# Attention, a gated feed-forward and a Fourier mix in one kernel: other PSUM slots in attention, another order of its first loads and copies, and a second pass without one-column matmuls

## The chip, the cores and the metric

The kernel runs on one core of a Trainium2 chip. The metric is the time of one execution on the device in microseconds (us), smaller being better. The engines are named as in the profile: PE is the matrix engine (TensorE), PEld its weight loads, DVE is VectorE, ACT is ScalarE, POOL is GpSimd, SP is the engine that issues most transfers. PSUM, into which PE writes, has eight banks here, and the kernel's PSUM tiles take one bank each.

## The reference

Three layers follow each other, with B, H, S, DH = 4, 12, 448, 64 and D = 768.

```python
scores = np.matmul(q, k.transpose(0, 1, 3, 2)) / np.sqrt(64) - np.log(S)
x = np.matmul(1.0 / (1.0 + np.exp(-scores)), v)         # then (B, S, D)
xk = mu_k * x + (1 - mu_k) * x_prev                     # x_prev: one token earlier
xr = mu_r * x + (1 - mu_r) * x_prev
kk = np.maximum(xk @ w_k, 0.0)                          # D -> 1024
x = sigmoid(xr @ w_r) * (kk * kk @ w_v)
u = x + np.real(np.fft.fft(np.fft.fft(x, axis=1), axis=2))
un = (u - mean(u)) / np.sqrt(var(u) + 1e-6)
out = u + np.maximum(un @ w_ch1, 0.0) @ w_ch2           # D -> 3072 -> D
```

## The kernel before, in words

The kernel writes one instruction order for every engine by hand. A planner (class `Order`) runs Python generators against a modelled clock `o.now`: a matmul adds its modelled cost to the clock, other engines have a modelled time at which they are free, and a generator that yields a time is resumed when the clock has come there. What a generator issues while it runs is the next instruction of its engine, and at run time each engine works through its list in that order, waiting where data or a buffer is missing. `o.others()` makes all generators that are due run before the calling one goes on, and lets no queued matmul in. Matmuls of the large products are put into `o.feed`, from which the planner takes one whenever no generator is due.

Attention works on 24 pairs of heads (`pairs`, six for each batch; `WHOLE` is 6). Per pair, `scores` makes seven PSUM tiles of 128 keys by 448 queries: six half blocks (numbers 0 to 5, contraction over 64 rows, so that two can share the array) and one full block (`FULL`, number 6). Each gets a sigmoid on ACT (`weigh`). One period later `attnv` adds up the values of the pair into one PSUM tile `av` (14 instructions of fp32 matmul), and `join` copies it to `x` on ACT, stores it, and makes from it the inputs of the key product (`mix`: an ACT scaling, a DVE step, an ACT cast `xkh`, a DVE subtraction `xkl`). Pairs 0 to 5 use fp32 matmuls for the scores; from pair 6 on q and k are split into two parts (`qh`, `ql`, `kh`, `kl`) and three fp32r matmuls make a block. Between the pairs, from pair 8 on, the key product of finished batches is fed in (`keys`, tiles of 18 matmuls, read by ACT's Relu, a square and a cast in `key_done`); a pace of 10.8 modelled us per pair leaves room for it. The planner issues `join` 0.2 modelled us after the last value matmul at the earliest; a score pair of fp32r matmuls is planned at 0.107 each.

PSUM slots turn in order of allocation: a tile waits until the last reader of the tile that had its slot is done. Before the change `ps1` has three slots, shared by key tiles, value sums and full blocks (`bank`), and `ps2` has five, for the half blocks (`room`). After attention `ps2` is given up and five slots (`ps1b`, `bank2`) take its place; `bank` goes on with its three slots.

The first transfers all go out on SP: `mu_k`, then k, q and v of pair 0, then the first weight and pair 1 (`load_mu`, `prepare`, `weights`).

The last layer's network runs over batches 0 and 1 first and then, in a second pass, over batches 2 and 3 together (`pair1`): for each of 12 groups of hidden units seven products of nine matmuls each, X, Y, Z, W, X, Z, W, in four PSUM tiles, and then the second matrix for both batches. In even groups the first product is preceded by an fp32 matmul over one column (`one` in `step`), into a column that nothing reads.

Of the kernel before, what the change touches and what calls it, by code (L numbers as in the profile page):

```python
# [12 lines left out]
F32 = mybir.dt.float32  # L13
# [4 lines left out]
PSUM = bass.MemoryType.PSUM  # L18
# [227 lines left out]
def build(tc, ap):  # L246
    nc = tc.nc
# [4 lines left out]
    def pool(stack, name, bufs=1, side="left", space=None):  # L252
        if space is not None:
            return stack.enter_context(tc.tile_pool(name=name, bufs=bufs, space=space))
        return stack.enter_context(tc.tile_pool(name=name, bufs=bufs, side=side, reuse_waits="tile"))
# [73 lines left out]
    t_d = {(nm, d): dram.tile([128, 2, S], F32, name=f"t_d{nm}{d}") for nm in LATE for d in range(3)}  # L329
    rs_d = [dram.tile([1, S], F32, name=f"rs_d{b}") for b in range(B)]  # L330

    ps1 = pool(est, "ps1", 3, space=PSUM)

    def bank(name):
        return ps1.tile([128, 512], F32, tag="bank", name=name)


# [3 lines left out]
    mop = pool(s_l, "mop", 2, "left")  # L341
    shift(mop, "mop")
    att = pool(s_r, "att", 2, "right")
    ps2 = pool(s_ps, "ps2", 5, space=PSUM)

    bias_s = wkp.tile([128, 1], F32, name="bias_s")
    V.memset(bias_s, -math.log(S))
# [8 lines left out]
    def prepare(what):  # L356

        for i, (b, p) in enumerate(pairs):
            if i > 1:
                yield from o.issued(("av", i - 2) if what == "v" else (what, i - 2) if i - 2 >= WHOLE else ("pair", i - 2))  # L360
            shape = {"k": [128, 4, 128], "q": [128, S], "v": [128, 4, 2, DH]}[what]
            raw = att.tile(shape, F32, tag=what, name=f"{what}_{i}", bufs=2)
            t = o.dma(raw, ap[what][b, p])
            if what == "v" or i < WHOLE:
                pair_t[what, i] = raw
                o.at[what, i] = t
                yield t
            else:
                yield t
                if i > WHOLE + 1:  # L370
                    yield from o.issued(("pair", i - 2))
                if what == "q" and i == WHOLE:
                    shift(att, "att")
                hi, lo = (att.tile(shape, F32R, tag=what + x, name=f"{what}{x}_{i}", bufs=2) for x in "hl")
                pair_t[what, i] = hi, lo
                yield o.act(hi, raw)
                o.at[what, i] = t = o.sub(V, lo, raw, hi)
                yield t
# [6 lines left out]
    def weigh(i, n, ps):  # L385
        sg = att.tile([128, S], F32, tag="sg", name=f"sg_{i}_{n}", bufs=len(places) + 1)
        o.at["sg", i, n] = o.act(sg, ps[:, 0:S], AF.Sigmoid, bias=bias_s, scale=1.0 / math.sqrt(DH))
        sg_t[i, n] = sg

    def scores(i):  # L390
        k, q = pair_t["k", i], pair_t["q", i]

        def rows(j):
            return slice(0, 128) if j is None else slice(64 * j, 64 * j + 64)

        def room(n):
            name = f"sc_{i}_{n}"
            return bank(name) if n == FULL else ps2.tile([128, 512], F32, tag="sc", name=name)

        if i < WHOLE:  # L400
            for n in [FULL, *range(FULL)]:
                c, j = places[n]
                ps = room(n)
                o.mm(ps[:, 0:S], k[rows(j), c], q[rows(j)], True, True, 0.760 if j is None else 0.447)
                weigh(i, n, ps)
                yield from o.others()
        else:
            halves = [(2 * c, 2 * c + 1) for c in range(3)]
            for ns in [(FULL,), *halves] if i < WHOLE + 2 else [*halves, (FULL,)]:
                ps = {n: room(n) for n in ns}  # L410
                for t, (a, b) in enumerate(((0, 0), (0, 1), (1, 0))):
                    for n in ns:
                        c, j = places[n]
                        cost = None if j is None else 0.107
                        o.mm(ps[n][:, 0:S], k[a][rows(j), c], q[b][rows(j)], t == 0, t == 2, cost)
                for n in ns:
                    weigh(i, n, ps[n])
                yield from o.others()
        o.at["pair", i] = o.now

    def attnv(i, ps):
        v = pair_t["v", i]
        for n in [FULL, *range(FULL)]:
            yield from o.need(("sg", i, n))
            c, j = places[n]
            sg = sg_t.pop((i, n))
            if j is None:
                o.mm(ps[:, 0:S], v[:, c].rearrange("p j d -> p (j d)"), sg, True, False, 0.760, skip=True)
            else:
                me = slice(64 * j, 64 * j + 64)  # L430
                o.mm(ps[me, 0:S], v[:, c, j], sg, False, c == 2, 0.432, skip=True)
            yield from o.others()
        o.at["av", i] = o.now
        o.spawn(join(i, ps), o.now + 0.2)
# [23 lines left out]
    def load_mu(mu, src):  # L458

        o.dma(mu[:, 0], src)  # L460
        o.ts(mu[:, 1], mu[:, 0], -1.0, 1.0, ALU.mult, ALU.add)

    def attention():
        for i in range(len(pairs) + 1):
            t0 = o.now
            if i > 0:
                yield from o.need(("v", i - 1), ("sg", i - 1, FULL))
                if i > 2:
                    yield from o.issued(("mixed", i - 3))
                yield from attnv(i - 1, bank(f"av_{i - 1}"))  # L470
            if i < len(pairs):
                yield from o.need(("k", i), ("q", i))
                yield from scores(i)
            yield t0 + pace()
        yield from o.need(("xk", B - 1, NP - 1))
        o.at["attention"] = o.now
# [55 lines left out]
        for part, every in zip((w_parts[:NF], w_parts[NF:]), EVERY):  # L532
            yield from load_split(att, part, raws=2, vector=True, every=every)

    load_mu(mu_k, ap["mu_k"])
    for what in "kqv":
        o.spawn(prepare(what))
    o.spawn(attention())
# [6 lines left out]


    ps1b = pool(est, "ps1b", 5, space=PSUM)

    def bank2(name):
        return ps1b.tile([128, 512], F32, tag="bank2", name=name)  # L550
# [599 lines left out]
    def network():  # L1150
# [31 lines left out]
        def pair1(g, _):  # L1182

            ps, t = {}, {}

            def tmp(nm):
                t[nm] = ws2.tile([128, S], F32, tag=nm, name=f"{nm}_{g}", bufs=1)
                return t[nm]

            def after(n):  # L1190
                x, y, z, w = (ps[k][:, 0:S] if k in ps else None for k in "XYZW")
                if n == 0:
                    o.at["c1", g] = o.act(tmp("u2"), x)
                elif n == 1:
                    yield from o.need(("c1", g))
                    o.at["u2", g] = o.tt(V, t["u2"], t["u2"], y, ALU.add)
                elif n == 2:
                    yield from o.need(("u2", g))
                    o.at["u3", g] = o.tt(V, tmp("u3"), t["u2"], z, ALU.add)
                elif n == 3:  # L1200
                    yield from o.need(("u3", g))
                    o.at["c22", g] = o.tt(V, t["u3"], t["u3"], w, ALU.add)
                    yield o.at["c22", g]
                    yield from hidden(g, 3, 1, t["u3"])
                elif n == 4:
                    yield from hidden(g, 2, 0, x)
                elif n == 5:
                    o.at["c21", g] = o.tt(V, tmp("c21"), t["u2"], z, ALU.add)
                    yield o.at["c21", g]
                    yield from hidden(g, 2, 1, t["c21"])  # L1210
                else:
                    yield o.tt(V, t["u2"], t["u2"], w, ALU.add)
                    yield from hidden(g, 3, 0, t["u2"])
                yield o.now

            def step(n, i, lhs, rhs, k):
                if i == 0 and n < 4:
                    ps[k] = (bank2 if k == "Y" else bank)(f"f1_{g}_{k}")
                if n == 0 and i == 0 and g % 2 == 0:
                    one = (ps[k][:, 511:512], lhs.bitcast(F32), rhs[:, 0:1].bitcast(F32))  # L1220
                    o.mm(*one, True, True, cost=0.2, skip=True)
                o.mm(ps[k][:, 0:S], lhs, rhs, i == 0 and n < 4, i == 8, skip=True)
                if i == 8:
                    o.at["prod", 7 * g + n] = o.now
                    o.spawn(after(n), o.now + 0.1)

            for n, (_, rows, k) in enumerate(PRODUCTS):
                blk = blk_t.get(7 * g + n)
                yield from o.need(("blk", 7 * g + n))
                yield from o.need(*((key, g) for key in {4: ["c1"], 5: ["u3"], 6: ["c22"]}.get(n, [])))  # L1230
                blk = blk_t[7 * g + n]
                for d in range(3):
                    yield from o.need(("t", rows, d))
                    ws = [blk[:, c : c + 128] for c in (128 * d, D // 2 + 128 * d)]
                    rs = [t_t[rows, d][:, c] for c in range(2)]
                    for i, (a, c) in enumerate(((0, 0), (0, 1), (1, 0))):
                        o.feed.append(partial(step, n, 3 * d + i, ws[a], rs[c], k))
                while len(o.feed) > 6:
                    yield o.now + 0.1
# [124 lines left out]
```

## Time and profile before

| | |
|---|---|
| runs before | 1208.70, 1209.18, 1209.23 us; median 1209.18 |
| the profiled execution | 1210.05 us, of which the span of the trace is 1208.3 |
| PE busy | 1198.8 us, 99% of the span, 6142 matmul records |
| DVE, ACT, POOL busy | 894.3, 483.0 and 53.8 us |
| DMA queue of SP | 214.37 MB, busy for 51.5% of 16 engines' span |
| attention and the keys behind it | PE's first matmul at 4.9 us to 282.4 us |
| receptance, values, spectrum, first pass | 282.4 to about 879 us |
| second pass | about 879 us to the end |

A row of the timeline gives the start and the time of an instruction (or of several alike, x n), its engine, its line, the operation, what it writes and reads with shapes, and in square brackets the idle time of its engine ahead of it and what ended that. Line numbers such as L181 are those of the planner's helpers, so groups are told apart by the names of tiles: `sc` scores, `sg` their sigmoids, `av` value sums, `x` their copies, `k` key tiles, `kt` what Relu and square make of them, `f_X` to `f_W` the products of the second pass. Matmuls are pipelined and their ends are modelled, so starts are more telling than ends: in a steady stream one starts every 0.20 us.

### The profile page before, as it was taken

The numbers are of one execution on the slowest core, as the hardware profiler recorded it, in microseconds if no ns is written. First come the engines' busy times: TensorE is split into PE (matmuls) and PEld (weight loads), VectorE is DVE, ScalarE is ACT, GpSimd is POOL, SyncE is SP. The second block draws the span as 40 slices with busy tenths as digits, with TensorE's granted clock in tenths as the row PEclk, the third lists the DMA queues.
The fourth block names the chain that finished last, engine by engine and source line by source line (L and its number), as shares of the span: only waits on it lengthen the run. The fifth ranks groups of instructions, "written<-read, shape, count | busy, mean of one in ns | idle before, by whom it ended". The sixth has DMA issues, their size and how long they took to land.

```text
span 1208.3 us, 16376 instructions
## 1 busy us (share of the span) xinstructions
PE 1198.8 (99%) x6142; PEld 1048.8 (87%) x6142; DVE 894.3 (74%) x1465; ACT 483.0 (40%) x864; POOL 53.8 (4%) x57
## 2 busy tenths in 40 slices
PE   8999999999999999999999999999999999999998
PEld 3467677689999999999999999999999999999998
DVE  5676887656862668797999989899567776777654
ACT  5877677657640121242333333333133332222320
POOL 0000000000000000000000000000021111211110
PEclk9999999999999999999999999999999999999999
DMA  6657569766957555386556555744942112121102
GB/s 213 215 181 233 199 234 349 258 228 237 302 204 246 199 168 199 120 292 239 188 198 212 199 206 196 244 172 177 366 144 79 53 53 79 53 69 63 53 1 92
DMA packets 77295, 217.81 MB, mean 180 GB/s; under 512 B 9312, under 2 KB 31776, under 8 KB 76576
## 3 DMA queue, kind: packets, MB, share of 16 engines
q1 hardware_dynamic: 76544, 214.37, 51.5%
q0 software_dynamic: 672, 2.40, 0.6%
q8 instruction: 48, 0.79, 0.3%
q14 instruction: 31, 0.25, 0.1%
HBM read 143.84 MB, written 72.90 MB: 179 GB/s over the span
## 4 chain that ended last, share of the span: by engine, by line
PE 98%; DMA 1%; ACT 0%; issue 0%; SPq 0%; DVE 0%
PE f L181 43%; PE k L181 10%; PE v L181 9%; PE r L181 7%; PE sc L181 7%; PE av L181 6%; PE f_X L181 4%; PE f_W L181 4%; PE f_Z L181 4%; PE f_Y L181 2%; PE pq L181 1%; DMA k<-k_d 1%; PE pa L181 1%; PE qa L181 1%; PE var L181 0%; DMA q<-in_q 0%
## 5 line engine op out<-in xcount | busy, mean ns | idle before, releaser
L216 DVE TENSOR_TENSOR acc<-acc,f 128x448 f32<-128x448 f32 x258 | 157.3, 617 | 60.3 <-PE f L181 57.6
L181 PE MATMUL f<-un,w1h 128*128 128x448 f32 x576 | 163.7, 364 | 0.0
L181 PE MATMUL f<-h,w2h 128*128 128x448 f32 x576 | 162.8, 363 | 0.0
L181 PE MATMUL f<-h,v2h 128*128 128x448 f32 x576 | 162.2, 362 | 0.0
L235 ACT ACTIVATE sg<-sc,bias_s 128x448 f32<-128x448 f32 x168 | 95.2, 651 | 61.0 <-PE sc L181 61.0
L224 DVE SCALAR_TENSOR_TENSOR w_bits<-w_raw,w_bits 128x768 uint32<-128x768 uint32 (+1 forms) x120 | 114.5, 954 | 1.7
L181 PEld LDWEIGHTS f<-un,w1h 128*128 128x128 f32 x576 | 108.1, 188 | 7.3 <-issue 0.4
L181 PEld LDWEIGHTS f<-h,w2h 128*128 128x128 f32 x576 | 108.0, 188 | 7.3 <-DVE acc L216 0.3
L181 PEld LDWEIGHTS f<-h,v2h 128*128 128x128 f32 x576 | 108.0, 188 | 6.9
L181 PE MATMUL v<-k,wvh 128*128 128x448 f32 x384 | 112.3, 366 | 0.6 <-DMA k<-k_d 0.6
L181 PE MATMUL f<-h,v2l 128*128 128x448 f32 x288 | 104.1, 361 | 0.0
L181 PE MATMUL f<-un,w1l 128*128 128x448 f32 x288 | 103.9, 361 | 0.0
L181 PE MATMUL f<-h,w2l 128*128 128x448 f32 x288 | 103.8, 360 | 0.0
L181 PE MATMUL av<-sg,v 128*64 128x448 f32 (+1 forms) x336 | 81.0, 549 | 0.0
L216 POOL TENSOR_TENSOR v2l<-v,v2h 128x768 fp32r<-128x768 f32 x24 | 46.4, 1950 | 748.5 <-ACT v2h L233 748.5
L181 PEld LDWEIGHTS v<-k,wvh 128*128 128x128 f32 x384 | 71.6, 188 | 6.6 <-DMA k<-k_d 1.3
L181 PE MATMUL v<-k,wvl 128*128 128x448 f32 x192 | 70.1, 365 | 0.0
L181 PE MATMUL k<-xkh,wkh 128*128 128x448 f32 x192 | 69.9, 364 | 0.0
L181 PE MATMUL k<-xkl,wkh 128*128 128x448 f32 x192 | 69.7, 363 | 0.0
L181 PE MATMUL k<-xkh,wkl 128*128 128x448 f32 x192 | 69.5, 362 | 0.0
L181 PEld LDWEIGHTS av<-sg,v 128*64 128x64 f32 (+1 forms) x336 | 27.8, 143 | 43.0 <-issue 36.5
L235 ACT ACTIVATE w_raw<-w_raw 128x768 f32<-128x768 f32 x40 | 36.8, 920 | 58.4 <-DVE w_bits L224 45.8
(174 smaller groups left out, 2254.2 us busy)
## 6 DMA issues: line engine op xcount, KB each, us to landing
w_raw<-in_w SPq DMA_DIRECT2D x40, 768.0 KB, 4.6
w_d<-w_bits SPq DMA_DIRECT2D x40, 384.0 KB, 2.6
k_d<-kp SPq DMA_DIRECT2D x32, 448.0 KB, 2.8
k<-k_d SPq DMA_DIRECT2D x32, 448.0 KB, 6.0
a<-w_d SPq DMA_DIRECT2D x24, 384.0 KB, 3.6
v<-w_d SPq DMA_DIRECT2D x24, 384.0 KB, 3.1
k<-in_k SPq DMA_DIRECT2D x24, 256.0 KB, 5.3
v<-in_v SPq DMA_DIRECT2D x24, 256.0 KB, 3.0
```

What stands on the lines that cost most here:

```text
L181: self.nc.tensor.matmul(out, lhs, rhs, start=start, stop=stop, skip_group_check=skip)
L216: eng.tensor_tensor(out, a, c, op=op)
L224: self.nc.vector.scalar_tensor_tensor(out, a, scalar, c, op0=op0, op1=op1)
L235: self.nc.scalar.activation(out, a, fn, **kw)
```

## The change

Three parts. In attention, PSUM is split as two slots (`ps1`) and six (`ps2`) and not three and five. The full blocks of pairs 6 to 23 and the value sums of pairs 6 to 23 go to the six; those of pairs 0 to 5 stay in the two, with the key tiles. After attention a one-slot pool `ps1c` gives `bank` its third slot back, and every third call of `bank` uses it. In pairs 6 to 23, `scores` calls `o.others()` once more, between the matmuls of blocks 0 and 1 and their sigmoids. At the start, q of pair 0 is issued on ACT's queue, and `mu_k` is loaded by a generator that is due at 2.5 modelled us, not before everything else. In the second pass the one-column matmuls are left out.

```diff
-    ps1 = pool(est, "ps1", 3, space=PSUM)
+    ps1 = pool(est, "ps1", 2, space=PSUM)
+    ps1c = []
+    banked = [0]
     def bank(name):
+        banked[0] += 1
+        if ps1c and banked[0] % 3 == 0:
+            return ps1c[0].tile([128, 512], F32, tag="bankc", name=name)
         return ps1.tile([128, 512], F32, tag="bank", name=name)
...
-    ps2 = pool(s_ps, "ps2", 5, space=PSUM)
+    ps2 = pool(s_ps, "ps2", 6, space=PSUM)
...
-            t = o.dma(raw, ap[what][b, p])
+            t = o.dma(raw, ap[what][b, p], nc.scalar if what == "q" and i == 0 else None)
...
+    def slot(name):
+        return ps2.tile([128, 512], F32, tag="sc", name=name)
...
-            return bank(name) if n == FULL else ps2.tile([128, 512], F32, tag="sc", name=name)
+            return bank(name) if n == FULL and i < WHOLE else slot(name)
...
                         o.mm(ps[n][:, 0:S], k[a][rows(j), c], q[b][rows(j)], t == 0, t == 2, cost)
+                if ns[0] == 0:
+                    yield from o.others()
                 for n in ns:
                     weigh(i, n, ps[n])
...
-                yield from attnv(i - 1, bank(f"av_{i - 1}"))
+                yield from attnv(i - 1, (bank if i <= WHOLE else slot)(f"av_{i - 1}"))
...
-    load_mu(mu_k, ap["mu_k"])
+    def first_mu():
+        load_mu(mu_k, ap["mu_k"])
+        yield o.now
+
+    o.spawn(first_mu(), 2.5)
...
     ps1b = pool(est, "ps1b", 5, space=PSUM)
+    ps1c.append(pool(est, "ps1c", 1, space=PSUM))
...
-                if n == 0 and i == 0 and g % 2 == 0:
-                    one = (ps[k][:, 511:512], lhs.bitcast(F32), rhs[:, 0:1].bitcast(F32))
-                    o.mm(*one, True, True, cost=0.2, skip=True)
```

## Rows read from the trace of the kernel before

**Rows 1.** The page: busy time of an engine, share of the span, instructions.

```profile
PE 1198.8 (99%) x6142; PEld 1048.8 (87%) x6142; DVE 894.3 (74%) x1465; ACT 483.0 (40%) x864; POOL 53.8 (4%) x57
```

**Rows 2.** Table by stage: stretch, its us, busy us per engine, PEclk, DMA share, GB/s.

```profile
0.00:10.00 10.00, 5.11 (x12) 2.35 (x14) 0.32 (x3) 3.07 (x4) 0.34 (x6) 1.00 0.75 238
120.00:160.00 40.00, 40.00 (x213) 27.53 (x213) 34.37 (x50) 28.26 (x57) 0.67 (x4) 1.00 0.58 196
160.00:200.00 40.00, 40.00 (x213) 29.04 (x212) 32.33 (x45) 30.04 (x59) 0.74 (x4) 1.00 0.88 307
251.60:282.40 30.80, 30.80 (x155) 28.88 (x155) 18.05 (x31) 20.61 (x39) 0.00 (x0) 1.00 0.65 241
581.00:879.00 298.00, 298.00 (x1492) 279.03 (x1491) 262.79 (x391) 100.97 (x147) 1.07 (x1) 1.00 0.62 218
```

**Rows 3.** Chain that ended last, pair 12: start, us, what.

```profile
113.46 3.22 PE sc L181 x21
116.67 5.01 PE k L181 x25
```

**Rows 4.** Timeline of PE's matmuls, scores of pair 12.

```profile
114.11 0.36 PE L181 MATMUL sc<-qh,kh 64*128 64x448 f32 x2
...
114.71 0.75 PE L181 MATMUL sc<-qh,kh 64*128 64x448 f32 x2
...
115.79 0.47 PE L181 MATMUL sc<-qh,kh 128*128 128x448 f32 x1
```

**Rows 5.** Timeline of weight loads: values of pair 6, scores of pairs 7 and 12.

```profile
56.20 0.28 PEld L181 LDWEIGHTS av<-sg,v 128*64 128x64 f32 x2 [0.47 <-ACT sg L235]
...
60.32 0.18 PEld L181 LDWEIGHTS sc<-qh,kh 64*128 64x128 f32 x1 [0.57 <-ACT sg L235]
...
114.99 0.18 PEld L181 LDWEIGHTS sc<-qh,kh 64*128 64x128 f32 x1 [0.30 <-ACT sg L235]
```

**Rows 6.** Who waited for whom, 60 to 251 us: total, times, longest.

```profile
PEld sc L181 <- ACT sg L235: 5.3, 17, 0.6
```

**Rows 7.** Timeline of ACT, first sigmoids of pair 12.

```profile
114.30 1.16 ACT L235 ACTIVATE sg<-sc,bias_s 128x448 f32<-128x448 f32 x2 [3.66 <-PE sc L181]
...
115.35 0.53 ACT L233 COPY x<-av 128x448 f32<-128x448 f32 x1
```

**Rows 8.** Timeline of all engines, a boundary between key tiles.

```profile
131.29 0.58 ACT L235 ACTIVATE kt<-k 128x448 f32<-128x448 f32 x1
...
131.89 0.36 PE L181 MATMUL k<-xkh,wkh 128*128 128x448 f32 x1
```

**Rows 9.** Timeline of all engines, the start and pair 2.

```profile
0.74 0.38 SPq L239 DMA_DIRECT2D mu_k<-in_mu_k  x1
...
0.95 1.28 ACT L235 ACT_TABLE_LOAD   x1 [0.95 <-DVE bias_s L347]
1.18 0.42 SPq L239 DMA_DIRECT2D k<-in_k  x1
1.65 0.42 SPq L239 DMA_DIRECT2D q<-in_q  x1
...
4.89 6.48 PE L181 MATMUL sc<-q,k 128*128 128x448 f32 x14 [4.89 <-DMA q<-in_q]
...
8.31 0.34 PEld L181 LDWEIGHTS sc<-q,k 64*128 64x128 f32 x2 [0.41 <-issue]
...
9.05 0.46 PEld L181 LDWEIGHTS sc<-q,k 64*128 64x128 f32 x2 [0.41 <-issue]
...
23.14 0.19 PEld L181 LDWEIGHTS sc<-q,k 64*128 64x128 f32 x2 [0.18 <-issue]
...
23.51 0.19 PEld L181 LDWEIGHTS sc<-q,k 64*128 64x128 f32 x2 [0.18 <-issue]
```

**Rows 10.** Chain that ended last, first products of groups 2 and 3.

```profile
926.03 2.03 PE f_X L181 x11
...
953.28 1.80 PE f_X L181 x9
```

## The prediction

> **What bounds the kernel now.** I read the busy table first: TensorE (PE) is busy for 1198.8 of 1208.3 us [rows 1]. So time comes back only if PE gets fewer instructions, starts earlier, or stands still less between instructions; the reader should see that the last kind can hide in "busy", because a matmul that is held up is drawn long. The table by stage says where to look [rows 2]: in the attention stage PE counts as fully busy, with VectorE (DVE) at 34.37 of 40 us and the DMA engines at 0.88 at their worst, so neither is full. The chain of waits then gives the score step of one pair as 3.22 us and the key feed between pairs as 25 matmuls in 5.01 us, so 0.20 each [rows 3].
>
> The score step is 18 half-height matmuls, which run two at a time, and 3 full ones. At 0.20 a step that is 12 steps, 2.4 us, plus what the changes of array shape cost. PE's timeline [rows 4] shows where the rest goes. Blocks 2 and 3 take 0.60 (114.11 to 114.71). Blocks 4 and 5 start at 114.71, but the next shape begins only at 115.79, 1.08 later. The weight loads tell why: the load for block 5 stood 0.30 us and was released by a sigmoid [rows 5]. Six half blocks turn through five slots, so block 5 takes the slot of block 0 of the same pair, and ScalarE (ACT) began block 0's sigmoid only at 114.30 [rows 7]. The list of waits has this wait 17 times from 60 to 251 us, 5.3 us in all [rows 6]: 16 pairs at 0.30 and pair 7 at 0.57 [rows 5].
>
> **The score slots, part by part.** In pairs 8 to 23 a pair now puts eight tiles through six slots: value sum, blocks 0 to 5, full block. Block 5 reuses the value sum's slot and the full block reuses block 0's. Block 5 is due at about 114.71. The copy of the value sum, which stood behind two sigmoids at 115.35 and took 0.53 [rows 7], is now put ahead of them: the planner resumes whatever is due at the new `others()`, and the copy's generator is due 0.2 after the last value matmul, while the first score pair is planned at 0.64. The value matmuls end about 113.46 [rows 3] and ACT then sat idle until 114.30 [rows 7], so the copy fits before the first sigmoid (113.46 + 0.53 = 114.0) and delays nothing; without that idle time it would push block 0's sigmoid by up to 0.53. The full block is due about 115.4 and block 0's sigmoid ends near 114.9, some 0.5 to spare. So the stall goes and no other takes its place in this step.
>
> What a stall is worth: at least the 0.30 that the load stood, at most 1.08 - 0.60 = 0.48, of which part is the change of shape that stays. I take 0.40, about the middle. Sixteen pairs: 6.4, between 4.8 and 7.7. Pair 7 stood 0.57 and is followed by keys, so PE can use the time: with the same 0.10 on top, 0.67. In pair 6 the value matmuls behind the scores wait for their sigmoids (0.47 in one load [rows 5]); ACT sets the pace there, and I give nothing. Pairs 0 to 5 keep full block and value sum in the two other slots: each pair's two tiles find the slots of the pair before, whose readers are done, so nothing. Attention together: 7.07.
>
> **Two slots for keys.** Keys had three slots together with value sums and full blocks, and now have two alone. Tile t+2 waits for the first ACT pass (Relu) over tile t. A tile is 18 matmuls (3.6 us) and a feed is 25, so only if a boundary falls in the first 7 matmuls of a feed does a third tile begin in the same feed: 7 of 18, some 6 feeds; elsewhere value sums and scores lie between. Behind the last pair the keys run on without a break, but there ACT is busy 20.61 of 30.80 us with no sigmoids ahead of Relu [rows 2], so nothing. The tightest one I found: Relu at 131.29 for 0.58, so done at 131.87, and the tile two later began at 131.89 [rows 8]. It is late because it queues behind the seven sigmoids and the casts. Taking the 0.53 copy out of that queue while PE gains 0.40 leaves it 0.13 better off; but an earlier copy also lets one more cast of the key inputs, about as long as that Relu, get ahead of it. Cost: nothing at best, 6 x 0.58 = 3.5 at worst. I take 0.4, one such wait, since only the tightest has no slack.
>
> **The start.** SP issues `mu_k` at 0.74, k at 1.18 and q at 1.65; PE's first matmul waited for q until 4.89, 3.24 after its issue [rows 9]. With `mu_k` behind v and q on ACT's own queue, k and q both go out near 0.74. With the same 3.24, PE starts at 3.98, 0.91 earlier. ACT's table load stood at 0.95 with nothing before it; q's issue is ahead of it in program order, and the first sigmoid is far off, so the load moves under cover. If the table load went first, q would leave at 0.95 + 1.28 = 2.23, 0.58 later than now: that is the bound below nothing. The SP loads behind q move up by one or two issues of about 0.45; no PE wait hangs on them. PE does not use the whole gain. Over 0 to 10 us the granted clock is listed as 1.00 [rows 2], yet weight loads step 0.74 there (8.31 to 9.05) against 0.37 later (23.14 to 23.51) [rows 9], the rate of the 1.2 GHz level against the 2.4 GHz one. If the end of the slow steps stays where it is, 0.91 is spent at half rate and is worth 0.45; if it moves with the start, 0.91. I take 0.6. The Trainium skill (TensorE: Matmul & The Clock Gate, Part 1, "What's actually happening") says that the cold stretch is a matter of time and not of a number of matmuls, and varies from run to run; by it I would take nearer 0.91 and the sum would be 0.3 larger. One trace cannot show it.
>
> **One-column matmuls.** In the second pass the first product of an even group is 11 instructions in 2.03 us where that of an odd group is 9 in 1.80 [rows 10]. The fp32 matmul over one column is the two more: 0.23 each, six groups, 1.38 us, on PE's path with no waits around it. Bounds: 0 if a wait takes their place, 1.38 if none does; I take 1.38, as the odd groups run without. The Trainium skill (TensorEngine Tiling (Array Packing), "Instruction Overhead") gives a one-column matmul the latency of a 60-column one, some 60 cycles; two of them at 2.4 GHz would be an estimated 0.05 us, six pairs 0.3, and the sum would be 1.1 smaller. The row includes their weight loads and decides.
>
> **Third slot of the later stages.** Every third call goes to the one-slot pool, two of three to the other: the same turn of three slots, so nothing, in either direction. The order of the later work follows PE's, so a shift of its start carries to the end.
>
> **Sum.** 7.07 + 0.6 + 1.38 - 0.4 = 8.65. The profiled execution took 1210.05 (span 1208.3 and 1.75 around it) and comes to 1201.4; the runs' median, 0.87 lower, comes to 1200.5.
>
> **Rivals.**
> - *The wait moves to ACT's queue.* Block 5 and the full block now hang on the copy and on sigmoid 0, keys on Relu. For: attention has only some idle ACT time, and a cast that waits for a load would, if pulled ahead of sigmoid 0, hold everything behind it. Against: 3.66 us of idle ACT ahead of the sigmoids in the pair read [rows 7]. If half the stalls come back and keys cost 1.3: 3.5 + 0.6 + 1.38 - 1.3 = 4.2, 1205.0.
> - *The score gain is not kept:* DVE or the loads set the attention stage and the stalls only covered for them. Against: DVE 34.37 of 40, which a 0.40 shorter 11.4 us pair makes 35.6. Then 0.6 + 1.38 = 2.0 is left: 1207.2.
> - *Slower: two key slots.* If Relu came late in all 6 feeds, the gain of 9.05 is eaten at 1.5 us a feed. Four ACT passes (two casts of the scores' inputs, scaling, cast of the key inputs) of about 0.6 could get ahead of Relu, 2.4 in all: 6 x 2.4 = 14.4 lost, 1209.18 - 9.05 + 14.4 = 1214.5. It needs all four ahead where most already are.
> - *The one-column matmuls keep the clock up.* Against: 298 us of the first pass without any, at 1.00 [rows 2]. Each us at the lower level costs 0.5; eating 8.65 needs 17 us of it.
> - *More than forecast:* all bounds at their best, 7.7 + 0.67 + 0.91 + 1.38 = 10.7: 1198.5.
>
> **How the numbers follow.** Forecast (1198.5 to 1203): 0.67. Wait moved (1203 to 1206.7): 0.18. Gain not kept (about 1207, within 0.2%): 0.05. Slower by keys or clock: 0.06. Still faster than 1198.5: 0.04. A measurement of this kernel tells 0.2%, 2.4 us, from no change. So faster 0.89, same 0.05, slower 0.06. The forecast's own bounds: 10.7 at best, and 4.8 + 0.57 - 0.58 + 1.38 = 6.2 at worst, 1203.0. To hold 8 in 10 it reaches into the first rival: 1198.0 to 1205.0.
>
> **What would show it.** Right: the score step of pairs 8 to 23 in 2.8 us, no load of scores released by a sigmoid, the copy ahead of the first sigmoid, key matmuls 0.20 apart across tile boundaries, PE's first matmul near 4.0, every first product 1.80. Wrong: a weight load of block 5 or the full block waiting for the copy or a sigmoid, a key load waiting for Relu, first matmul at 5 or later, slow steps in the second pass, or DVE full through attention.

## The result, and the profile after

Six runs of the changed kernel gave a median of 1199.85 us (1199.50 to 1200.44), six of the kernel before on the same chip 1209.51 (1208.70 to 1210.97): a ratio of 0.9919, with a 95% interval of 0.9907 to 0.9932. The forecast was 1200.5. The profiled execution took 1199.81 (span 1198.0) where that of before took 1210.05 (1208.3), so the two spans differ by 10.3 and the medians by 9.7. What may have made the 0.6 between them is told with the start of the kernel, below.

The busy table of the page after answers to [rows 1]: PE is still 99% of the span, and the 10 us are missing from its own busy time, not from its idle time.

```profile
PE 1188.8 (99%) x6130; PEld 1043.9 (87%) x6130; DVE 894.2 (75%) x1465; ACT 484.8 (40%) x864; POOL 54.0 (5%) x57
```

The table by stage, for stretches that answer to [rows 2]. DVE and the DMA engines carry the same work in less time; in the 40 us from 120 they rise to 35.86 us and to 0.67 and are still not full. The last row is the second pass: without its one-column matmuls it keeps a granted clock of 1.00.

```profile
0.00:10.00 10.00, 5.49 (x15) 2.15 (x15) 1.79 (x5) 3.72 (x6) 0.34 (x6) 1.00 0.79 273
120.00:160.00 40.00, 40.00 (x223) 29.97 (x224) 35.86 (x51) 33.00 (x64) 0.29 (x3) 1.00 0.67 223
...
870.20:1197.00 326.80, 324.05 (x1620) 303.33 (x1618) 222.94 (x374) 87.02 (x160) 45.51 (x24) 1.00 0.20 65
```

The chain that ended last, after (start, us, what). It answers to [rows 3, 9, 10]: the score step of pair 12 is 2.82 where it was 3.22, the key feed behind it is unchanged, the score step of pair 2 is 3.41, and the first product of the first even group of the second pass is 9 instructions in 1.80.

```profile
0.74 3.73 DMA q<-in_q
4.51 5.47 PE sc L181 x14
9.99 3.35 PE av L181 x14
...
20.17 3.41 PE sc L181 x14
...
43.92 4.36 PE av L181 x14
48.27 2.82 PE sc L181 x21
...
55.43 2.82 PE sc L181 x21
...
108.96 2.82 PE sc L181 x21
111.78 5.01 PE k L181 x25
...
122.77 5.12 PE k L181 x25
...
870.17 1.80 PE f_X L181 x9
```

The same chain before, where it is read below: the scores of pairs 2 and 5, the values of pair 5, the scores of pair 7 from 57.69 to 61.19.

```profile
21.78 3.65 PE sc L181 x14
...
42.78 4.17 PE sc L181 x14
46.95 3.59 PE av L181 x14
...
57.69 0.84 PE sc L181 x3
...
61.19 3.61 PE k L181 x17
```

And from its weight loads the one in pair 5 that stood 0.47 for a sigmoid:

```profile
45.93 0.29 PEld L181 LDWEIGHTS sc<-q,k 64*128 64x128 f32 x2 [0.47 <-ACT sg L235]
```

The timeline of pair 12 after, beside [rows 4, 5, 7]. The copy of the value sum now runs at 109.33, ahead of the first sigmoid at 109.80. Blocks 4 and 5 load both their weights at 110.01 without a wait, run two at a time from 110.20, and the full block begins at 110.91: 0.71 behind them, where it was 1.08. The 0.30 that is left ahead of the full block's load has no releaser; it is the change of array shape. The copy began 0.37 us behind the scores, not at once, and ended as the first sigmoid began; that one came 0.84 behind the start of the scores, as before. So the copy fitted, with less to spare than the prediction says.

```profile
109.33 0.54 ACT L233 COPY x<-av 128x448 f32<-128x448 f32 x1 [3.08 <-PE av L181]
109.80 2.74 ACT L235 ACTIVATE sg<-sc,bias_s 128x448 f32<-128x448 f32 x5
110.01 0.19 PEld L181 LDWEIGHTS sc<-qh,kh 64*128 64x128 f32 x2
110.20 0.37 PE L181 MATMUL sc<-qh,kh 64*128 64x448 f32 x2
110.90 0.19 PEld L181 LDWEIGHTS sc<-qh,kh 128*128 128x128 f32 x1 [0.30 <-issue]
110.91 0.47 PE L181 MATMUL sc<-qh,kh 128*128 128x448 f32 x1
```

The list of waits from 60 to 251 us, after (who, for whom: total, times, longest). The row of [rows 6], loads of scores waiting for a sigmoid, is gone. One load of scores waited for a copy and one load of keys for Relu (`kt`), each once. The load is the first one of pair 22, behind keys; 0.30 is what the full block's load above stands too, with no releaser, and the score step of that pair is 2.83, so nothing was lost by it.

```profile
PEld sc L181 <- ACT x L233: 0.3, 1, 0.3
...
PEld k L181 <- ACT kt L235: 0.2, 1, 0.2
```

**The account.** Cutting both chains at the same pieces of work gives where the 10.3 us of span came from:

| stretch (before, after) | before | after | gain |
|---|---|---|---|
| start to the value sums of pair 0 | 11.37 | 9.99 | 1.38 |
| to the scores of pair 6 (50.54, 48.27) | 39.17 | 38.28 | 0.89 |
| scores and values of pair 6, scores of pair 7 (61.19, 58.25) | 10.65 | 9.98 | 0.67 |
| to the keys behind the last pair (251.60, 242.63) | 190.41 | 184.38 | 6.03 |
| those keys (282.41, 273.44) | 30.81 | 30.81 | 0.00 |
| receptance to the first pass (878.97, 870.17) | 596.56 | 596.73 | -0.17 |
| second pass, to the end of the span | 329.33 | 327.83 | 1.50 |

One pair of traces holds some scatter; the twelve traces of this document tell more. From the value sums of pair 0 to the end of the keys, the three kernels with the old slots and the old copy take 270.99 to 271.04 us, and the four with the new slots, the copy ahead and the casts as they were 263.40 to 263.45: 7.6 for the slots and the call together, where the forecast had 7.07 less 0.4. The new slots without the copy ahead take 268.92, the copy ahead with the old slots 271.51. The second pass takes 329.29 to 329.33 in three traces with one-column matmuls and 327.83 to 327.92 in nine without. The stretch between the two, where the kernels differ only in the pools of their three `bank` slots, takes 596.39 to 597.82 (596.49 to 597.01 with the old slots), so -0.17 is scatter, and part of the scatter of the medians comes from there.

### The profile page after: what moved, and what is told of

Its sections match the earlier page's. It is cut to its first block, busy times and chain, and to the rows that moved or that the text cites. A ratio compares the mean times of both kernels' runs of the same rounds, so it can differ in the third digit from the quotient of the medians.

```text
span 1198.0 us, 16329 instructions
## 1 busy us (share of the span) xinstructions
PE 1188.8 (99%) x6130; PEld 1043.9 (87%) x6130; DVE 894.2 (75%) x1465; ACT 484.8 (40%) x864; POOL 54.0 (5%) x57
## 4 chain that ended last, share of the span: by engine, by line
PE 98%; DMA 1%; ACT 0%; DVE 0%; issue 0%; SPq 0%
PE f L181 43%; PE k L181 10%; PE v L181 9%; PE r L181 7%; PE av L181 6%; PE sc L181 6%; PE f_X L181 4%; PE f_Z L181 4%; PE f_W L181 4%; PE f_Y L181 2%; PE pq L181 1%; DMA k<-k_d 1%; PE pa L181 1%; PE qa L181 1%; PE var L181 0%; DMA q<-in_q 0%
```

## The experiments

| kernel | median, us | before beside it | ratio, 95% interval |
|---|---|---|---|
| slots without the copy moved ahead | 1205.73 | 1209.76 | 0.9969 (0.9959 to 0.9980) |
| copy ahead, old slots | 1210.43 | 1209.76 | 1.0007 (0.9997 to 1.0017) |
| one-column matmuls out, nothing else | 1208.55 | 1209.76 | 0.9990 (0.9980 to 0.9999) |
| new start, nothing else | 1209.40 | 1209.76 | 1.0000 (0.9991 to 1.0010) |
| changed kernel, q on SP | 1200.41 | 1209.34 | 0.9924 (0.9909 to 0.9939) |
| changed kernel, `mu_k` first | 1200.47 | 1209.34 | 0.9926 (0.9911 to 0.9941) |
| changed kernel, casts on DVE | 1198.65 | 1209.34 | 0.9914 (0.9899 to 0.9928) |
| changed kernel, matmuls of zeros first | 1198.46 | 1209.34 | 0.9908 (0.9892 to 0.9925) |
| casts on DVE and matmuls of zeros | 1196.85 | 1210.26 | 0.9893 (0.9878 to 0.9908) |
| the same, q on SP | 1197.61 | 1210.26 | 0.9893 (0.9877 to 0.9910) |

**The slots without the copy ahead.** The changed kernel without its new `o.others()`.

```diff
-                if ns[0] == 0:
-                    yield from o.others()
                 for n in ns:
```

> The changed kernel without the new others() call, so the value sums share the six score slots but are copied behind the first two sigmoids as before. Theory (a slot's last reader decides): from pair 8 on block 5 waits for the copy, which stands behind two sigmoids and ends about 2.5 us after the scores begin; the score step grows from 2.82 to about 4.1 us, 16 pairs lose some 1.3 us each, about 1220 us, slower than before. Rival (the sixth slot alone pays, the order of the copy is a detail): score step 2.82, about 1200 us. In pairs 1 to 5, whose scores use six slots as well, both expect the score step of the changed kernel, 3.41 us and not 3.65.

The score steps of pairs 8 to 21 took 3.20 to 3.21, those of pairs 22 and 23 took 2.82 and 2.81; so neither 4.1 nor 2.82 for all. Those of pairs 1 to 5 took 3.40 to 3.41, as expected. In the timeline of pair 12 of this kernel, block 5's load at 112.53 is still released by a sigmoid, and the copy begins only at 112.90 and ends at 113.44:

```profile
111.85 1.16 ACT L235 ACTIVATE sg<-sc,bias_s 128x448 f32<-128x448 f32 x2 [3.65 <-PE sc L181]
...
112.53 0.18 PEld L181 LDWEIGHTS sc<-qh,kh 64*128 64x128 f32 x1 [0.29 <-ACT sg L235]
...
112.90 0.54 ACT L233 COPY x<-av 128x448 f32<-128x448 f32 x1
...
113.34 0.19 PEld L181 LDWEIGHTS sc<-qh,kh 128*128 128x128 f32 x1 [0.31 <-ACT sg L235]
```

Block 5 at 112.53 and the full block at 113.34 both began before the copy had ended, so neither took the value sum's slot; block 5 still hung on sigmoid 0. That contradicts what the text ahead of the prediction says, that slots turn in order of allocation, and neither expectation came true. What fits is that a slot is handed on in the order in which the last readers are issued: without the new call the first two sigmoids are issued ahead of the copy, and blocks 0 and 1 are first in line. The banks in the programs built from the kernels bear it out: in pairs 8 to 21 of this kernel block 5 has the PSUM bank of block 0 and the full block that of block 1, and in pairs 8 to 23 of the changed kernel they have those of the value sum and of block 0. Pairs 22 and 23 of this kernel show the same from the other side: keys come between value sums and scores there, so the copy is issued first without the new call, block 5 has the value sum's bank, and the step is 2.82. In pair 22 the copy runs ahead of the scores, which begin at 225.09:

```profile
224.18 0.54 ACT L233 COPY x<-av 128x448 f32<-128x448 f32 x1 [0.81 <-issue]
```

So in 14 pairs the sixth slot alone leaves the stall where it was, 14 times 0.39 or 5.5 us, of the 5.9 by which the medians of this kernel and the changed one differ. Pairs 1 to 5, 7, 22 and 23 gain by the slots without the call.

**The copy ahead with the old slots.** The kernel before with the new `o.others()`.

```diff
+                if ns[0] == 0:
+                    yield from o.others()
                 for n in ns:
```

> The kernel before with the new others() call alone: value sums copied ahead of the first sigmoids, three and five slots. Theory: the copy moves into time in which ScalarE stood idle, block 5 still waits for the sigmoid of block 0, so score steps stay 3.2 us and the time stays within 1 us of before (1209.5). Rival (the earlier copy pays by itself): score steps 2.8, about 1203 us.

The copy did move, to 113.30, ahead of the sigmoids, and nothing was gained: in the timeline block 5's load still waits for sigmoid 0, since there are still five slots for six half blocks, and in the chain the score step stays 3.21.

```profile
113.30 0.54 ACT L233 COPY x<-av 128x448 f32<-128x448 f32 x1 [3.19 <-PE av L181]
...
114.72 0.18 PEld L181 LDWEIGHTS sc<-qh,kh 64*128 64x128 f32 x1 [0.29 <-ACT sg L235]
```

So for pairs 8 to 21 each half of the change gives nothing alone, and both together give the whole stall. In the changed kernel the call decides two things: when the copy runs, and who gets its slot.

**The one-column matmuls alone.** The kernel before without them.

```diff
-                if n == 0 and i == 0 and g % 2 == 0:
-                    one = (ps[k][:, 511:512], lhs.bitcast(F32), rhs[:, 0:1].bitcast(F32))
-                    o.mm(*one, True, True, cost=0.2, skip=True)
```

> The kernel before without the six one-column matmuls, nothing else. Theory: each first product of an even group falls from 2.03 to 1.80 us, 1.4 us in all, about 1208.1. By the rule of 60 cycles a small matmul only 0.3 us, about 1209.2. Rival (they keep the clock up): a granted clock under 1.00 or steps over 0.20 us in the second pass, and a time above 1209.5.

The median fell by about 1.2, with an interval of 0.1 to 2.4, less than the 2.4 that a measurement of this kernel tells from no change. The chain of this kernel tells it: the second pass begins at 877.93 with a first product of 1.80 and lasts 327.9 to the end of its 1205.8 us span, against 329.33 before. The rival did not show: nine matmuls in 1.80 are steps of 0.20, and the granted clock of the second pass is 1.00.

```profile
877.93 1.80 PE f_X L181 x9
```

**The start alone.** The kernel before with q of pair 0 on ACT's queue and `mu_k` late.

```diff
-            t = o.dma(raw, ap[what][b, p])
+            t = o.dma(raw, ap[what][b, p], nc.scalar if what == "q" and i == 0 else None)
...
-    load_mu(mu_k, ap["mu_k"])
...
+    o.spawn(first_mu(), 2.5)
```

> The kernel before with q of pair 0 on ScalarE's queue and mu_k loaded later, nothing else. Theory: first matmul at 4.5 and not 4.9 us, slow steps end about 1 us earlier too, value sums of pair 0 start at about 10.0 and not 11.4, and the whole runs 1.4 us shorter, about 1208.1. Rival (what is gained at the start is lost in a wait further on): value sums of pair 0 earlier but the time within 0.5 us of 1209.5.

Nothing that can be measured: the median is 0.4 lower, where 1.4 was expected, and the value sums of pair 0 begin at 10.38, where 10.0 was. Its chain has the first matmul at 4.56. Three traces have the start of before: the kernel before, the one with only the copy moved and the one without one-column matmuls. Their first matmul is at 4.89, 4.79 and 4.71, their value sums of pair 0 begin at 11.37, 10.59 and 10.02. Four traces have the new start (this one, the changed kernel, the slots without the copy, the casts on DVE): first matmul at 4.51 to 4.58, value sums at 9.99 to 10.48. So the first matmul comes 0.1 to 0.4 earlier, but the starts of the value sums overlap, and a gain behind the first scores, 0.4 on the means, is not shown. Most of the 1.38 in the account is scatter: the trace of before has the slowest first scores of all, 6.48, where the other two with its start have 5.80 and 5.31.

```profile
4.56 5.82 PE sc L181 x14
10.38 3.35 PE av L181 x14
```

**q on SP.** The changed kernel with q issued on SP right behind k, `mu_k` still late.

```diff
-            t = o.dma(raw, ap[what][b, p], nc.scalar if what == "q" and i == 0 else None)
+            t = o.dma(raw, ap[what][b, p])
```

> The changed kernel with q of pair 0 back on SP, behind k, and mu_k still late. Theory (the order of issue is what counts, not the second queue): q goes out at 1.18, and with the 3.24 us from issue to first matmul of the kernel before PE starts near 4.4, as early as with ScalarE's queue (4.51); time within 0.6 us of the changed kernel (1199.85). Rival (the second queue pays): first matmul at 4.9.

The chain shows q issued at 1.18, 0.44 later than on ACT's queue, and landed at 3.97, 0.50 earlier: 2.79 from issue to landing and not 3.73. The median is the same within 0.6. So the second queue buys nothing here; it is enough that q is no longer third on SP, behind `mu_k` and k, where three traces have the first matmul at 4.71 to 4.89.

```profile
1.18 2.79 DMA q<-in_q
4.11 5.30 PE sc L181 x14
```

**`mu_k` first again.** The changed kernel with q on ACT's queue and `mu_k` ahead of k on SP.

```diff
...
-    o.spawn(first_mu(), 2.5)
+    load_mu(mu_k, ap["mu_k"])
```

> The changed kernel with mu_k issued first again and q still on ScalarE's queue. Theory: k goes out at 1.18 and not at 0.74, lands some 0.4 us later, and PE waits for k: first matmul near 4.8; time 0 to 0.5 us above the changed kernel. Rival (only q's issue matters): first matmul at 4.5.

The expected 4.8 was a miss, and so was the rival's 4.5: PE began at 4.28, held by k and no longer by q, as both landed sooner after their issue than in the changed kernel (the last section has the numbers). The first scores took 5.05. Over the three new orders PE starts between 4.11 and 4.58, and with the new slots their medians are 1199.85 to 1200.47: which of them is taken moves less than can be measured here.

```profile
1.18 2.97 DMA k<-in_k
4.28 5.05 PE sc L181 x14
```

**Casts on DVE.** In the chain after, the values of pair 5 take 4.36 where those of pairs 0 to 4 take about 3.4, and around pair 6 the chain runs through ACT. In this kernel DVE makes the casts `qh` and `kh` of pairs 6 and 7, and ACT those of the later pairs.

```diff
-                yield o.act(hi, raw)
+                if i < WHOLE + 2:
+                    V.tensor_copy(hi, raw)
+                    yield o.spend(V, 0.07 + o.size(hi) * 0.00104)
+                else:
+                    yield o.act(hi, raw)
```

> The changed kernel with the casts qh and kh of pairs 6 and 7 on VectorE and not on ScalarE. Theory (ScalarE sets the pace of the value sums of pairs 5 and 6): value sums of pair 5 in 3.4 and not 4.36 us, pair 6 from scores to the end of its value sums some 0.5 us shorter, together about 1.5 us: 1198.4. Rival (the casts now queue behind VectorE's weight passes of 0.96 us, and the scores of pairs 6 and 7 wait for them): no gain, 1199.9 or more.

The chain of this kernel: the values of pair 5 take 3.37 (0.99 less) and those of pair 6 take 3.82, where from the end of pair 6's scores to the start of pair 7's it was 4.34 (51.09 to 55.43). That is 1.5 together. The medians differ by 1.2, but the two ratios' intervals overlap, so the traces have to tell it: from the value sums of pair 0 to the end of the keys this kernel and the two later ones with these casts take 262.12 to 262.16, where the changed kernel and the three like it take 263.40 to 263.45. The casts on DVE are worth 1.3.

```profile
44.16 3.37 PE av L181 x14
...
50.35 3.82 PE av L181 x14
54.16 2.83 PE sc L181 x21
```

**Matmuls of zeros first.** The changed kernel with two fp32 matmuls of a zeroed tile, while q is on its way, into the tile that the first scores then overwrite. Each is two records.

```diff
+    zero = wkp.tile([128, S], F32, name="zero")
+    V.memset(zero, 0.0)
...
+                if i == 0 and n == FULL:
+                    for _ in range(2):
+                        o.mm(ps[:, 0:S], zero[:, 0:128], zero, True, True, 0.02)
```

> The changed kernel with two fp32 matmuls of a zeroed tile into the first score tile, issued before q lands; the first real matmul overwrites what they wrote. Theory (the slow steps end a while after PE has begun to work): PE begins near 1.5, the first score matmul still comes at about 4.5, and the scores of pair 0 take 3.4 to 4 us and not 5.5; 1.5 to 2 us gained, about 1198.1. Rival (the end of the slow steps lies at a fixed time, or work on zeros does not count): scores of pair 0 at 5.5, time as the changed kernel or later, where the zero matmuls end after q lands.

The first real scores still begin at 4.57, and the value sums of pair 0 at 8.40, 1.59 earlier than in the changed kernel. The timeline shows why: the zeros' weight loads step 0.75, the half rate, and the loads of the half blocks at 6.73 and 7.10 already step 0.37.

```profile
1.42 3.35 PE L181 MATMUL sc<-zero 128*128 128x448 f32 x4 [1.42 <-DVE zero L355]
2.33 0.33 PEld L181 LDWEIGHTS sc<-zero 128*128 128x128 f32 x1 [0.41 <-issue]
3.08 0.33 PEld L181 LDWEIGHTS sc<-zero 128*128 128x128 f32 x1 [0.41 <-issue]
4.57 3.83 PE L181 MATMUL sc<-q,k 128*128 128x448 f32 x14
...
6.73 0.19 PEld L181 LDWEIGHTS sc<-q,k 64*128 64x128 f32 x2 [0.18 <-issue]
7.10 0.19 PEld L181 LDWEIGHTS sc<-q,k 64*128 64x128 f32 x2 [0.18 <-issue]
```

The median is 1.4 below that of the changed kernel, but the intervals of the two ratios overlap. In the changed kernel's timeline the steps are 0.74 until the load at 8.70 and 0.37 behind it:

```profile
7.96 0.34 PEld L181 LDWEIGHTS sc<-q,k 64*128 64x128 f32 x2 [0.41 <-issue]
8.70 0.19 PEld L181 LDWEIGHTS sc<-q,k 64*128 64x128 f32 x2 [0.40 <-issue]
9.07 0.19 PEld L181 LDWEIGHTS sc<-q,k 64*128 64x128 f32 x2 [0.19 <-issue]
```

**Both, and both with q on SP.** The last two edits together, and then with q behind k on SP (the diff of the q run).

> Changed kernel with both of the last two edits: casts of the split inputs of pairs 6 and 7 on DVE, and two fp32 matmuls of a zeroed tile ahead of the first scores. The zero tile is work that the reference does not have. Theory (the two gains lie at different places, the first us and pairs 5 and 6, and nothing sits between them that could absorb either): the gains add, 1.2 from the casts and 1.4 from the earlier matmuls, so about 1197.2, ratio near 0.990. Value sums of pair 0 begin near 8.4, value sums of pair 5 take 3.4. Rival (the two gains were mostly scatter from run to run, since the start alone varies by about 1 us): 1198.5 again, and the two chain numbers move only one at a time.

> The kernel of the run with casts on DVE and matmuls of a zeroed tile, with q of pair 0 issued on SP behind k instead of on ACT's queue. Theory (once the first steps run at the full rate, each us that q lands earlier is a us off the end): q landed near 4.0 with this order and near 4.5 with the other, so 0.4 less: first real score matmul at 4.1, value sums of pair 0 near 8.0, about 1196.8. Rival (the slow steps end at a fixed time after the first matmul, so an earlier q only moves more scores into the slow part): first real score matmul at 4.1, value sums of pair 0 at 8.2 to 8.4, time within 0.2 of the other kernel.

The first gave 1196.85, close to the 1197.2 expected, and its interval against before, 0.9878 to 0.9908, lies almost wholly below that of the changed kernel. It has the lowest median here; the next kernel has the same ratio. Its profiled execution, at 1198.70, was the slowest of its four runs (the others 1196.21 to 1196.93). The chain of that execution has the values of pair 5 in 3.37, as expected, but, by its timeline, the first real scores in 4.53 (the value sums of pair 0 begin at 9.10 and not at 8.4), and the longest stretch from the end of the keys to the second pass of all twelve traces, 597.82, whose work no edit of this run touches:

```profile
1.42 7.68 PE sc L181 x18
```

In the second k had landed by 4.14, where its first weight load starts, but the real scores began at 4.57 all the same, as the matmuls of zeros, 4 records from 1.42, held PE until then. The expected 4.1 was a miss, and so were the value sums of pair 0, expected near 8.0 and by the rival at 8.2 to 8.4: they began at 9.39, where the kernel with q on SP and no zeros has 9.41. So in this trace the zeros gained nothing: they held PE until 4.57, where that kernel began its scores at 4.11. The ratio to before is that of the other kernel, 0.9893.

## Why the prediction was right, step by step

- **Score slots, 7.07.** Measured 6.98. The 16 steps of pairs 8 to 23 went from between 3.20 and 3.22 to 2.82, 0.39 on average, 6.3 in all; pair 7's step went from 3.50 (57.69 to 61.19) to 2.82, 0.68 where 0.67 was said; pair 6 gave nothing, as said. The 0.40, chosen about halfway between the load's 0.30 and the stretch of 0.48, was right to 0.01; no row had fixed it within these bounds, so that it came so near is luck. What the 6.3 lost on its way to the 6.03 of the account is one value step of 3.28 instead of 3.16, the key feed below, and a few hundredths.
- **Why it works.** The step in the text was wrong in its general form and right for this kernel: block 5 gets the value sum's slot because the new call issues the copy first, not because the value sum was allocated first (the first run and the banks show it). The prediction credited the call with getting the copy out of the way in time; the first run shows that without it the slot goes to another tile and 5.5 of the gain stay away.
- **Pairs 0 to 5, nothing.** Wrong by 0.89. The step looked only at where the full block and the value sum go. The half blocks of these pairs had also turned through five slots and got a sixth, and their score steps went from 3.65 to 3.41, that of pair 5 from 4.17 to 3.40; so they do with the slots alone, and not with the call alone. [rows 6] starts at 60 us and could not show that stall. The trace of before has a load of pair 5, at 45.93, standing 0.47 for a sigmoid. The five steps gave 1.80; 0.77 of it was lost again at once in the values of pair 5 (3.59 to 4.36) and the rest in the values of the pairs before; in pair 5 sigmoids and casts on ACT set the pace, as the run with casts on DVE shows.
- **Two key slots, 0.4 lost.** Measured 0.11: one feed of 5.12 where others take 5.01, with a wait of 0.2 for Relu. One late Relu, as said, shorter than said. No sign of the rival with six feeds of 1.5. The worst case of the forecast, 6.2, had left out the 3.5 that this step gave as its own worst; the outcome did not need it.
- **The start, 0.6.** The first step of this term was wrong. The forecast of the first matmul, 3.98, came out as 4.51: the step let q keep the 3.24 from its issue to the first matmul, but it took 3.77, as q, issued at the same moment as k, landed 3.73 after its issue (the last section). The start alone moved the median by nothing that can be measured, and 0.4 on the means of three and four traces, less than their scatter. In the two traces compared it shows as 1.38, as the first 14 score matmuls took 6.48 in the one and 5.47 in the other; over nine traces without matmuls of zeros they took 5.05 to 6.48. That is enough to account for the 0.6 by which the spans differ more than the medians; that it is the cause is not shown, as the stretch behind the keys scatters by 1.4 over the twelve traces as well.
- **Whether slow steps end sooner when PE starts sooner.** In two of three traces. With zeros from 1.42 on, the loads step at the full rate from 5.87, 7.06 and 7.72; in the nine traces without zeros from 7.67 at the earliest. So in two traces work on zeros counted as work, and the third cannot tell. The 14 real score matmuls took 3.83, 4.53 and 4.82 with zeros, all less than the nine without, but in the third they also began later than the data allowed. Whether 0.4 us of an earlier start moves the end, which is what the 0.6 rested on, is lost in this scatter. Over 0 to 10 us the granted clock is listed as 1.00 in the traces with zeros too, so only the steps of the loads show it. The rule of the Trainium skill (TensorE: Matmul & The Clock Gate, Part 1, "What's actually happening") is that the cold stretch is a matter of time and not of a number of matmuls, and varies from run to run. The traces agree that it varies; they do not separate time from number.
- **One-column matmuls, 1.38.** Measured 1.50 in the changed kernel and 1.46 alone, and 1.37 to 1.50 between any two of the twelve traces, so about 0.24 for each. The figure of the Trainium skill (TensorEngine Tiling (Array Packing), "Instruction Overhead"), by which the six would be an estimated 0.3, does not hold for an fp32 matmul of one column with its two weight loads. No clock was lost without them, which was a rival: the granted clock of the second pass after is 1.00.
- **Sum.** The terms as measured, 6.98 + 0.89 - 0.12 - 0.11 + 0.4 + 1.50 - 0.17, come to 9.4, where 8.65 was forecast; the 0.4 of the start is the uncertain one. What was missed is the 0.89 and 0.3 of the key slots on one side, the start and a few tenths of scatter on the other, so in part the total is near because errors cancel, which is luck too. The medians differ by 9.7, and the ratio's interval (8.2 to 11.2 us) holds both.

## What to carry to other kernels

A buffer more helps only the tile that gets it: when tiles of several kinds share a pool, look at the order in which their last readers are issued, since moving one reader ahead can be the half of the change without which the other half is worth little. Price a stall by the length of the step it sits in, between the load's own wait and the whole stretch, and look for the same stall in every stage that uses the pool, also where the list of waits you read did not begin yet. While PE waits for its first data, matmuls of zeros may shorten its slow first steps, as in two of three traces here, if they do not hold PE past the landing of the data. Compare starts over several traces before crediting an edit with them, and find a stretch that leaves the scatter out, as the one from the first value sums to the end of the keys does here.

## What the runs showed of the hardware

Two loads issued at the same moment on two queues each took longer to land than two issued 0.44 us or more apart. In six traces q went out on ACT's queue at 0.74, in the same moment as k on SP: q took 3.6 to 3.8 us from issue to landing and k 3.5 to 3.6. In the kernel with `mu_k` (3 KB) first again q went out on the same queue at the same time, but k 0.44 later: q took 2.8 and k 3.0. Behind k on SP q took 2.8 to 2.9 in two traces, and third on SP 2.9 to 3.1 in three. So it is not the second queue that goes with the longer time, but k beside it. The transfers issued in the first 2.2 us, of the changed kernel and then of the one with `mu_k` first (KB each, us to landing):

```profile
k<-in_k SPq DMA_DIRECT2D x1, 256.0 KB, 3.5
...
q<-in_q ACTq DMA_DIRECT2D x1, 224.0 KB, 3.7
```

```profile
k<-in_k SPq DMA_DIRECT2D x1, 256.0 KB, 3.0
...
q<-in_q ACTq DMA_DIRECT2D x1, 224.0 KB, 2.8
```

The first 14 score matmuls, always the same work, took between 5.05 and 6.48 us over nine traces, a scatter of 1.4 us, as much as the one-column matmuls cost.
